# A fixed table of order and engines in place of a list scheduler, in a fused attention and MLP kernel

## The chip, the cores and the metric

The kernel runs on one core of one Trainium2 chip. The metric is the device time of one execution in microseconds (us). An execution can fall in a slow state, more than 1.5% above the fastest run of the same kernel; only fast runs are compared here.

The names used: PE is the matrix engine, DVE, ACT and POOL are the vector, scalar and general engines, SP is the engine that here only issues DMAs. Each engine works through its own instructions in the order in which the program emitted them. In the lines of the profile, `qk` is q and k as loaded, `qkb` their cast, `qkT` the transpose; `pm`, `pt` and `px` are products with w_phi, `EB`, `ea` and `eax` their exponentials, `m` and `mx` maxima; `kv` and `num` are products of attention, `hT_ps` and `ch_ps` the two products of the MLP. PSUM is the memory that takes PE's products.

## The reference

Linear attention with a feature map of exponentials, then a LayerNorm MLP with a residual. Cut to what matters:

```python
# q, k, v: 8 batches x 8 heads x 576 x 64;  w_phi: 64 x 128
def phi(x):
    proj = x @ w_phi
    proj = proj - max(abs(proj))                    # over the 128 features
    return concat(exp(proj), exp(-proj))
kv, z = phi(k).T @ v, phi(k).sum(over s)
x = (phi(q) @ kv) / (phi(q) @ z + 1e-6)             # heads side by side: 8 x 576 x 512
xn = (x - mean(x)) / sqrt(var(x) + 1e-6) * g_ln
out = x + relu(xn @ w_ch1) @ w_ch2                  # 512 -> 2048 -> 512
```

## The kernel before

The work is cut into 32 units (one head of a pair of batches, or a like amount of two heads in the first pair) and the MLP of four pairs of batches. For the first 8 units q and k are transposed on PE; for the other 24 they are cast to bf16 on one of three engines and transposed by a DMA that SP issues. All of it is written as 2513 small operations, each with the engines that may do it, a guessed time on each, and the keys that it reads and writes:

```python
# one unit of pairs 1 to 3: the cast, then the DMA transpose
def cast(e):
    u["qkb"] = att.tile([P, 2, MX * D], BF16, tag="qkb", name="qkb")
    copy_on(e, u["qkb"], qk_bufs[g % NBUF][:, :, u["uu"], :])
def turn():
    u["qkT"] = att.tile([P, 1024], BF16, tag="qkT", name="qkT", bufs=NQ)
    nc.sync.dma_start_transpose(out=..., in_=...)                          # cut
add_any({"POOL": 1.0, "ACT": 0.95, "DVE": 0.8}, V, cast,
        r=main_keys(u, "k") + main_keys(u, "q"), w=[("qkb", n % 2)])        # two buffers
add("SP", 1.27, V, turn, r=[("qkb", n % 2)], w=[("turn", n), *ks], ...)

# MLP: the relu that empties PSUM has two engines, the scaling of w1 by g_ln one
add_any({"ACT": 0.08 + cols * 0.32 / 384, "DVE": 0.08 + cols * 0.4 / 384}, V - 30.0,
        relu, r=[key], w=[hkey[r, jj]], release=[("B", 1)])
add("DVE", 0.9, rank, emit, r=["gln"], w=[("w1", n, kc) for kc in range(KC)])
```

The list scheduler runs the operations through a small simulation with those guessed times and emits them in the order, and on the engines, that come out:

```python
class Order:
    def due(self): ...     # backward pass: gives each operation its rank
    def run(self):         # forward pass, cut
        while events:
            now = events[0][0]
            ...
            for engine, queue in waiting.items():
                if free[engine] > now + 1e-9 or not queue:
                    continue
                ...        # the operation of best rank whose buffers are free
                us = op.alts[engine]
                free[engine] = now + us
                done.append((op, engine))
                ...
        for op, engine in done:
            if op.emit:
                op.emit(engine)
```

Two things follow. An operation with several engines goes to one of them when the program is built. And the two `qkb` buffers are used in turn, so a cast must wait until the transpose of two units earlier has read its buffer; while it waits, everything behind it on its engine waits too. The Trainium skill ("TensorE: Matmul & The Clock Gate", Architectural detail) says that ACT and DVE are strict FIFO; the traces here agree, with a clear case in the experiments (in e5, DVE idle for 4.52 us ahead of a cast that waited for its load).

Of the kernel before, what the change touches and what calls it, by code (L numbers as in the profile page):

```python
# [3 lines left out]

# [16 lines left out]
    return dataclasses.replace(ap, ap=new_ap)  # L21


LAG = {"PE": 0.24, "DVE": 0.20, "ACT": 0.23, "POOL": 0.22, "SP": 0.1, "DMA": 1.8, "CAST": 1.8}


STAY = 10.0


class Op:  # L30
    __slots__ = (
        "alts", "emit", "rank", "lag", "users", "acquire", "release",
        "ready", "left", "number", "rows", "taken", "at", "early",
    )


class Order:


    def __init__(self, room):  # L40
        self.ops, self.wrote, self.read, self.room = [], {}, {}, dict(room)

    def add(
        self, alts, rank, emit, r=(), w=(), acquire=None, release=None, lag=None, rows=False,
        early=0.0
    ):
        op = Op()
        op.alts, op.emit, op.rank, op.lag = alts, emit, rank, lag
        op.early = early
        op.acquire, op.release, op.rows, op.taken = acquire, release, rows, False  # L50
        op.number, op.users, op.ready, op.at = len(self.ops), [], 0.0, None
        deps = {self.wrote[k].number: self.wrote[k] for k in (*r, *w) if k in self.wrote}
        for k in w:
            deps.update({o.number: o for o in self.read.get(k, ())})
        for o in deps.values():
            o.users.append(op)
        op.left = len(deps)
        for k in w:
            self.wrote[k], self.read[k] = op, []
        for k in r:  # L60
            self.read.setdefault(k, []).append(op)
        self.ops.append(op)
        return op

    def due(self):

        waiting, free, events = {}, {}, []
        before, left, ready = {}, {}, {}
        for op in self.ops:
            left[op.number], ready[op.number] = len(op.users), 0.0  # L70
            for o in op.users:
                before.setdefault(o.number, []).append(op)
            for engine in op.alts:
                waiting.setdefault(engine, [])
                free.setdefault(engine, 0.0)
            if not op.users:
                heapq.heappush(events, (0.0, op.number, op))
        rank, taken = {}, set()
        while events:
            now = events[0][0]  # L80
            while events and events[0][0] <= now + 1e-9:
                op = heapq.heappop(events)[2]
                if op is not None:
                    for engine in op.alts:
                        heapq.heappush(waiting[engine], (-op.rank, -op.number, op))
            for engine, queue in waiting.items():
                if free[engine] > now + 1e-9:
                    continue
                op = None
                while queue and op is None:  # L90
                    op = heapq.heappop(queue)[2]
                    if op.number in taken:
                        op = None
                if op is None:
                    continue
                taken.add(op.number)
                end = now + op.alts[engine]
                free[engine], rank[op.number] = end, -end
                heapq.heappush(events, (end, -1, None))
                for o in before.get(op.number, ()):  # L100
                    lag = max(LAG[e] for e in o.alts) if o.lag is None else o.lag
                    same = len(o.alts) == 1 and engine in o.alts
                    n = o.number
                    ready[n] = max(ready[n], end + (0.1 if same else lag))
                    left[n] -= 1
                    if not left[n]:
                        heapq.heappush(events, (ready[n], n, o))
        for op in self.ops:
            op.rank = rank[op.number] - op.early

    def run(self):
        waiting, free, room, events, done = {}, {}, self.room, [], []
        rows = False

        def offer(op):
            heapq.heappush(events, (op.ready, 1, op.number, op, None))

        for op in self.ops:
            for engine in op.alts:
                waiting.setdefault(engine, [])  # L120
                free.setdefault(engine, 0.0)
            if not op.left:
                offer(op)
        now = 0.0
        while events:
            now = events[0][0]
            while events and events[0][0] <= now + 1e-9:
                _, kind, _, op, _ = heapq.heappop(events)
                if kind == 1:
                    for engine in op.alts:  # L130
                        key = op.ready if engine in ("DMA", "CAST") else op.rank
                        heapq.heappush(waiting[engine], (key, op.number, op))
                elif kind == 0:
                    for name, n in op.release or ():
                        room[name] += n
            for engine, queue in waiting.items():
                if free[engine] > now + 1e-9 or not queue:
                    continue
                passed, held, op = [], set(), None
                if engine == "PE" and rows:  # L140
                    near = sorted(i for i in queue if i[2].rows and not i[2].taken)
                    near = [i for i in near if room[i[2].acquire[0]] >= i[2].acquire[1]]
                    if near and near[0][0] < queue[0][0] + STAY:
                        op = near[0][2]
                while queue and op is None:
                    item = heapq.heappop(queue)
                    op = item[2]
                    if op.taken:
                        op = None
                        continue  # L150
                    if op.acquire is None or (
                        op.acquire[0] not in held and room[op.acquire[0]] >= op.acquire[1]
                    ):
                        break
                    held.add(op.acquire[0])
                    passed.append(item)
                    op = None
                for item in passed:
                    heapq.heappush(queue, item)
                if op is None:  # L160
                    continue
                op.taken, op.at = True, (now, engine)
                if op.acquire:
                    room[op.acquire[0]] -= op.acquire[1]
                us = op.alts[engine]
                if engine == "DMA" and free.get("CAST", 0.0) > now:
                    shared = free["CAST"] - now
                    us = 4.0 * us if 4.0 * us <= shared else us + shared * 0.75
                end = now + us
                if engine == "PE" and op.rows != rows:  # L170
                    rows = op.rows
                    end += 0.1
                lag = LAG[engine] if op.lag is None else op.lag
                free[engine] = end
                done.append((op, engine))
                heapq.heappush(events, (end, 2, op.number, op, None))
                heapq.heappush(events, (end + lag, 0, op.number, op, None))
                for o in op.users:
                    same = len(o.alts) == 1 and engine in o.alts
                    o.ready = max(o.ready, end + (0.1 if same else lag))  # L180
                    o.left -= 1
                    if not o.left:
                        offer(o)
        assert len(done) == len(self.ops)
        for op, engine in done:
            if op.emit:
                op.emit(engine)
        return now


@with_exitstack
def kernel(
# [64 lines left out]
    sched = Order({"B": 8, "S": 8})  # L257
# [336 lines left out]
    def a_side(u, i, V):  # L594
# [10 lines left out]
        def em():  # L605
            if i:
                t_ = u["emk_g"]
            elif u["pair"]:
                t_ = u["emq_g"]
            else:  # L610
                if uu == 0:
                    t_ = att_sm.tile([P, 2, NT], FP32, tag="emq", name="emq")
                    group_units(g)[0]["emq_g"] = group_units(g)[1]["emq_g"] = t_
                t_ = u["emq_g"]
# [6 lines left out]
        w = [("em", i, n % 3)]  # L621
# [632 lines left out]
                pass  # L1254
    ET = mybir.EngineType
    with tc.manual_schedule(engines={ET.PE, ET.DVE, ET.Activation, ET.Pool, ET.SP}):
        sched.due()
        sched.run()


# [28 lines left out]
```

## Time and profile before

| | before |
|---|---|
| time, median of 4 runs | 377.43 us (376.82 to 377.68) |
| PE busy | 349.1 us, 93% |
| DVE / ACT / POOL busy | 273.1 / 257.5 / 182.4 us |
| PE idle, 0 to 100 us | 17.1 us (82.90 busy) |
| PE idle, 100 to 360 us | 4.6 us (255.38 busy) |

The page of the kernel before: its span, the busy time of each engine, and the clock and DMA rows of its 40 slices (each 9.4 us long).

```profile
span 375.2 us, 9069 instructions
...
PE 349.1 (93%) x3306; PEld 208.0 (55%) x3348; DVE 273.1 (73%) x738; ACT 257.5 (69%) x650; POOL 182.4 (49%) x349
...
PEclk9998799999999999999999999999999999999998
DMA  6999699999969745493547754712200244010102
```

(This trace lacks 42 matmul records, 36 of them between 100 and 360 us, so PE's busy time in it is a little low.)

### The profile page before, as it was taken

The page shows a single profiled execution, that of the slowest core. Times are in us where ns is not written, and L with a number is a line of the kernel's source. Part 1 is how long each engine was busy: PE and PEld are TensorE (multiplying, and loading weights), DVE is VectorE, ACT ScalarE, POOL GpSimd, SP SyncE. Part 2 cuts the span into 40 slices and gives each one's busy share as a digit, 9 for nine tenths or more (in the row PEclk, how much of TensorE's full clock was granted, in tenths as well). Part 3 has the DMA queues.
Part 4 walks back from the last instruction along what each step waited for, and adds up shares of the span by engine and source line. Part 5 has one row for each costly group of instructions (what it writes and reads, how often), then busy time and mean ns, then how long its engine had stood idle before and what let it go on. Part 6 is the DMA issues. An engine that isn't in the chain of part 4 may idle for free.

```text
span 375.2 us, 9069 instructions
## 1 busy us (share of the span) xinstructions
PE 349.1 (93%) x3306; PEld 208.0 (55%) x3348; DVE 273.1 (73%) x738; ACT 257.5 (69%) x650; POOL 182.4 (49%) x349
## 2 busy tenths in 40 slices
PE   2888789989999899999999999999999999999995
PEld 1466456546565555655656555655565546555553
DVE  3889989979879999987879979978788672000102
ACT  3889698799879648876569768966589437433310
POOL 5589989367866434744455537454447320000000
PEclk9998799999999999999999999999999999999998
DMA  6999699999969745493547754712200244010102
GB/s 174 291 281 192 124 223 265 239 233 234 256 145 242 221 114 119 84 237 106 189 141 159 208 130 99 152 39 72 66 2 28 58 114 98 9 48 29 56 30 84
DMA packets 89132, 52.43 MB, mean 140 GB/s; under 512 B 55552, under 2 KB 84608, under 8 KB 89088
## 3 DMA queue, kind: packets, MB, share of 16 engines
q1 hardware_dynamic: 84240, 47.11, 50.9%
q0 software_dynamic: 4224, 4.19, 7.0%
q10 hardware_dynamic: 624, 0.56, 0.5%
q8 instruction: 26, 0.43, 0.5%
q14 instruction: 18, 0.15, 0.1%
HBM read 36.77 MB, written 9.44 MB: 123 GB/s over the span
## 4 chain that ended last, share of the span: by engine, by line
PE 74%; DVE 9%; DMA 6%; ACT 6%; issue 2%; POOL 2%; SPq 0%; DVEq 0%; POOLq 0%
PE ch_ps L1033 30%; PE hT_ps L1001 29%; DMA qkT<-qkb 4%; PE num L738 4%; PE kv L709 4%; PE pm L580 3%; ACT EB L631 3%; DVE m L600 3%; DMA qk<-in_k_dram 2%; ACT ea L684 1%; PE pt L678 1%; DVE numc L744 1%; DVE numc L750 1%; PE kv L704 1%; DVE st L881 1%
## 5 line engine op out<-in xcount | busy, mean ns | idle before, releaser
L1001 PE MATMUL hT_ps<-xT,w 128*128 128x384 bf16 x768 | 150.7, 328 | 1.5 <-DVE m L600 1.0
L1033 PE MATMUL ch_ps<-w,hT 128*128 128x512 bf16 (+2 forms) x550 | 141.0, 373 | 2.7 <-issue 0.9
L1001 PEld LDWEIGHTS <-w 128*128 128x128 bf16 x768 | 71.4, 98 | 54.7 <-issue 5.2
L1011 ACT ACTIVATE hT<-hT_ps 128x384 bf16<-128x384 f32 x119 | 58.5, 496 | 58.9 <-PE hT_ps L1001 58.4
L600 DVE TENSOR_REDUCE m<-pm 128x4 f32<-128x512 f32 x128 | 81.4, 676 | 9.0 <-PE pm L580 8.9
L762 POOL TENSOR_TENSOR x<-numc,rden 128x192 bf16<-128x192 f32 (+1 forms) x112 | 50.4, 461 | 67.4 <-DVE rden L756 65.2
L1033 PEld LDWEIGHTS <-hT 128*128 128x128 bf16 x592 | 53.3, 98 | 47.0 <-issue 2.5
L684 ACT ACTIVATE ea<-pt 128x512 bf16<-128x512 f32 x128 | 69.0, 637 | 7.2 <-PE pt L678 7.1
L631 ACT ACTIVATE EB<-pm 128x512 bf16<-128x512 f32 x128 | 69.0, 634 | 3.0 <-DVE m L600 2.6
L1041 DVE SCALAR_TENSOR_TENSOR o<-ch_ps,rstd,x 128x512 f32<-128x512 f32 (+2 forms) x37 | 26.6, 727 | 54.6 <-PE ch_ps L1033 39.5
L645 POOL TENSOR_TENSOR vv<-v,emk 128x512 bf16<-128x512 f32 x32 | 33.5, 1047 | 43.9 <-ACT emk L616 33.3
L1009 DVE TENSOR_SCALAR hT<-hT_ps 128x384 bf16<-128x384 f32 x73 | 39.0, 542 | 4.9 <-PE hT_ps L1001 4.3
L744 DVE TENSOR_TENSOR numc<-num,emq 128x195 f32<-128x195 f32 (+1 forms) x96 | 32.4, 344 | 10.1 <-PE num L738 8.9
L738 PEld LDWEIGHTS <-ea 128*128 128x128 bf16 x512 | 28.0, 99 | 13.7 <-issue 1.9
L750 DVE TENSOR_TENSOR numc<-numc,num 128x195 f32<-128x195 f32 (+1 forms) x100 | 33.1, 342 | 1.2
L645 POOL TENSOR_TENSOR vv<-v,en 128x512 bf16<-128x512 f32 x32 | 33.5, 1047 | 0.0
L738 PE MATMUL num<-KV,ea 128*128 128x65 bf16 x512 | 31.8, 196 | 1.1 <-ACT ea L684 0.9
L881 DVE BATCH_NORM_STATS2 st<-x 128x6 f32<-128x512 bf16 x36 | 24.4, 677 | 2.1 <-POOL x L762 1.9
L709 PE MATMUL kv<-vv,EB 128*128 128x65 bf16 x512 | 25.0, 199 | 0.0
L580 PEld LDWEIGHTS <-qkT 64*128 64x128 bf16 x512 | 16.8, 99 | 14.2 <-issue 8.2
L890 ACT ACTIVATE xc<-x,mv 128x512 bf16<-128x512 bf16 x19 | 13.8, 725 | 14.6 <-DVE mv L882 12.2
L709 PEld LDWEIGHTS <-EB 128*128 128x128 bf16 x512 | 22.6, 102 | 1.6
(71 smaller groups left out, 371.3 us busy)
## 6 DMA issues: line engine op xcount, KB each, us to landing
out_dram<-o SPq DMA_DIRECT2D x31, 256.0 KB, 2.4
qk<-in_k_dram SPq DMA_DIRECT2D x28, 256.0 KB, 4.6
v<-in_v_dram SPq DMA_DIRECT2D x28, 256.0 KB, 3.7
qk<-in_q_dram SPq DMA_DIRECT2D x26, 256.0 KB, 5.2
w<-in_moe_w_ch_dram POOLq DMA_DIRECT2D x8, 512.0 KB, 9.4
qk<-in_k_dram SPq DMA_DIRECT2D x2, 512.0 KB, 6.8
qk<-in_q_dram SPq DMA_DIRECT2D x2, 512.0 KB, 7.8
v<-in_v_dram SPq DMA_DIRECT2D x2, 512.0 KB, 8.2
```

Of the source, the lines that this page charges most:

```text
L600: nc.vector.reduce_max(out=u["m", i].rearrange("p (c e) -> p e c", e=2)[:, e], in_=u["pm", i, e], axis=AX.X, apply_absolute_value=True,)
L631: nc.scalar.activation(u["EB"][:, t, e * 4 : (e + 1) * 4].rearrange("p c f -> p (c f)"), u["pm", 1, e].rearrange("p c f -> p (c f)"), AF.E ...
L645: nc.gpsimd.tensor_tensor(out=u["vv"][:, t, 0:MX, 0:D], in0=vb[:, uu, :].rearrange("p (c d) -> p c d", d=D), in1=bcast(e[:, 0:MX], 2, D), ...
L684: nc.scalar.activation(u["EA"][:, t, e * 512 : (e + 1) * 512], u["pt", e], AF.Exp, scale=(1.0, -1.0)[t],)
L709: nc.tensor.matmul(ps[:, t, c // 4, :], EB[:, t, (c % 2) * 4 + c // 2, :], vv[:, t, c, :], start=False, stop=(t == 0 and c == MX - 1), ski ...
L738: nc.tensor.matmul(ps[:, t, i, :], lhsT, rhs, start=(j == 0), stop=(j == len(terms) - 1))
L750: nc.vector.tensor_add(out=st["numc"][:, 0:nch], in0=st["numc"][:, 0:nch], in1=st["ps"][:, 0])
L762: nc.gpsimd.tensor_tensor(out=dst, in0=st["numc"][:, i : i + cnt, 0:D], in1=bcast(st["rden"][:, i : i + cnt], 2, D), op=ALU.mult,)
L1001: nc.tensor.matmul(st["ps"][:, 0:cols], w1_sb[:, kc, jj * P : (jj + 1) * P], pr["xT", r][:, kc, 0:cols], start=(kc == 0), stop=(kc == KC - 1),
L1009: nc.vector.tensor_relu(h_sb[:, 0:cols], st["ps"][:, 0:cols])
L1011: nc.scalar.activation(h_sb[:, 0:cols], st["ps"][:, 0:cols], AF.Relu)
L1033: nc.tensor.matmul(ch[t, c0], hT[r, jj][:, rt * P : (rt + 1) * P], w2_sb[:, jj, c0:c1], start=(jj == 0), stop=(jj == JC - 1),)
```

## The change

The intent: a search that was done offline found an order and a choice of engines that are better than what the list scheduler finds while the kernel is built; they are written down as a table and followed. A word of the table is the number of an operation, with a letter for the engine (d, a, p for DVE, ACT, POOL) where it has a choice.

```diff
 class Op:
-    __slots__ = ("alts", "emit", "rank", "lag", "users", ...)
+    __slots__ = ("alts", "emit", "number", "before")
 class Order:
-    def due(self): ...
-    def run(self): ...
+    def follow(self, order):
+        done = set()
+        for number, engine in order:
+            op = self.ops[number]
+            assert op.before <= done and engine in op.alts, number
+            if op.emit:
+                op.emit(engine)
+            done.add(number)
+        assert len(done) == len(self.ops)
+
+WORK = """
+0 6 1 2 4 10 8 7 12 3 5 11 14 9 59 16 13 60 18 36 61a 37 20 15 17 62a 69 19 22 21 78 70 23
+...                                                     (2513 words in all, cut)
+"""
@@ in the maxima of the first pair
-                if uu == 0:
+                if "emq_g" not in u:
@@ at the end
-        sched.due()
-        sched.run()
+        sched.follow(work(sched.ops))
```

Operations and dependences are the same 2513 in both. The edit of the maxima only lets either unit of a group be the first to take the group's tile.

## The prediction

> **What bounds the kernel now.** TensorE, but not everywhere. The page gives PE 349.1 us busy of 375.2 (93%), DVE 273.1, ACT 257.5, POOL 182.4. Busy time by windows of 12.5 us splits this: from 100 to 362 us PE is busy 11.7 to 12.5 of each, bound by its own work. From 12.5 to 62.5 us it is busy 9.9 to 11.6, while ACT (11.8, 11.7, 9.0, 11.6) and DVE (10.4, 11.7, 11.0, 12.5) are nearly full: attention's exponentials and maxima set the pace, and the first MLP matmul starts at 45.5 us (timeline of PE). Counting matmuls at their dense spacing (162 ns for 384 columns, 216 ns for 512, from the timeline) I estimate that PE loses 47 us between its first and last matmul: 25.6 before 45.5, 4.4 to 62.5, 8.9 to 125 (single waits of about 1.1 us near 52, 82 and 124 us), 8.0 after that, mostly 0.3 us at attention pieces that any order pays. Outside stand 3.5 us before the first matmul and 4.3 after the last.
>
> **What the change does.** Nothing is removed or added: the same 2513 operations and dependences, emitted in a table's order. With both orders side by side, PE's is a local shuffle of the old one (attention progress per MLP work is the same within about 1 us). Engine choices move: 8 of the 24 bf16 casts of q and k go from ACT or DVE to POOL, as do 7 centerings; 38 of 73 relus of DVE go to ACT, 27 come back. At durations near the trace's (relu 496 ns on ACT, 542 on DVE) DVE loses about 6 us of work, POOL gains 7, ACT is unchanged.
>
> **On the critical path.** Little before 45.5 us: the work ordered ahead of the first MLP matmul even grows (DVE 33.3 to 35.7 us, ACT 33.6 to 35.2, POOL 26.0 to 29.6), so it should start at 45 to 47.5 us. Ahead of the last third of the first pair's MLP DVE's share falls from 82.7 to 78.2 us, where DVE is 96% full: worth up to 4 us, at most the PE loss there. I count 1.5 us gained to 62.5, 3.5 from there to 125, 2 after: 7 us. The MLP end is already dense; the tail of 4.3 us is unchanged.
>
> A side condition is the clock: the windows show 0.86 and 0.73 granted in 25 to 50 us. The Trainium skill ("TensorE: Matmul & The Clock Gate", the HAM clock gate) says that the clock is halved after an idle window of about 3.4 us, free-running; this trace agrees in form (half clock for 3.4 and 6.8 us). A denser early PE may save, a shifted one lose, 1 to 3 us.
>
> **Predicted: 370.5 us**, 365.5 to 376 eight times in ten. Faster by over 2%: 0.42; within 2%: 0.54; slower: 0.04.
>
> **What would show it.** PE busy share 94 to 95%; DVE busy about 267, POOL about 189; PE's waits at 75 to 88 and 112 to 125 us shrunk; first MLP matmul no earlier than 45 us; last 60 us unchanged.
>
> **What would make it wrong.** A table tuned on a model that misses POOL's or the PSUM rotation's real waits would turn its tight order into stalls (slower). If the search also advanced the first MLP matmul by several us, the gain exceeds 10 us.

## More of the kernel before

PE is nearly full after 100 us, so what can still be won lies in the first quarter, where the DMA row stands at 9 as well.

The view by windows (busy time and count of PE, PEld, DVE, ACT and POOL, granted clock, DMA share, GB/s) splits that quarter:

```profile
70.00:75.00 5.00, 4.71 (x38) 2.27 (x37) 4.93 (x13) 4.84 (x10) 2.22 (x3) 1.00 0.93 254
75.00:88.00 13.00, 11.28 (x138) 6.88 (x137) 10.91 (x28) 11.97 (x32) 8.79 (x16) 1.00 1.14 234
```

From 70 to 88 us PE idles for 2.0 us while ACT is busy for 16.8 of 18. The chain of waits in that stretch shows with what (start, length, what):

```profile
61.53 10.27 DMA qkT<-qkb
...
71.82 1.04 ACT qkb L289
...
72.97 0.93 ACT qkb L289
73.91 0.98 ACT EB L631 x2
...
75.10 4.91 DMA qkT<-qkb
80.00 1.92 issue
81.93 0.86 DVE qkb L291
```

Two casts (`qkb`) take 2 us of ACT ahead of the exponentials (`EB`). A third sits on DVE. The timelines of DVE and PE there:

```profile
81.93 0.86 DVE L291 CAST qkb<-qk 128x1024 bf16<-128x1024 f32 x1 [1.92 <-issue]
82.71 1.01 DVE L1009 TENSOR_SCALAR hT<-hT_ps 128x384 bf16<-128x384 f32 x2
83.31 0.96 PE L947 MATMUL xT_ps<-ident,xc 128*128 128x128 bf16 x12 [0.91 <-DVE hT L1009]
```

Before its cast DVE sits idle for 1.92 us, until the transpose that reads this cast's buffer has landed (issued at 75.10, landed at 81.85, behind loads of q, k and v; the profile names no releaser, "issue"), two relus come late behind it, and PE waits 0.91 us for them. Last, the start of PE:

```profile
3.53 0.61 PE L550 MATMUL qkT_ps<-ident,qk 128*128 128x128 bf16 x4 [3.53 <-DMA qk<-in_k_dram]
5.67 0.61 PE L550 MATMUL qkT_ps<-ident,qk 128*128 128x128 bf16 x4 [1.53 <-DMA qk<-in_q_dram]
6.95 0.61 PE L580 MATMUL pm<-wbk,qkT 64*128 64x128 bf16 x8 [0.68 <-ACT qkT L289]
```

## The result, and the profile after

| | before | after |
|---|---|---|
| time, median of 4 runs | 377.43 us (376.82 to 377.68) | 373.21 us (372.68 to 374.35) |
| ratio | | 0.9895, 95% interval 0.9868 to 0.9922: within 2% |
| PE idle, 0 to 100 us | 17.1 us | 13.9 us (86.10 busy) |
| PE idle, 100 to 360 us | 4.6 us | 3.0 us (256.98 busy) |

A ratio here is the mean time of one kernel's fast runs over the mean of the other's fast runs of the same rounds, so it is not quite the ratio of the medians that stand beside it. The fall from 4.6 to 3.0 us after 100 us is not read as a gain, since the trace before lacks records there and the one after lacks none. The page after:

```profile
span 371.1 us, 9107 instructions
...
PE 349.6 (94%) x3348; PEld 208.1 (56%) x3348; DVE 266.8 (72%) x728; ACT 257.5 (69%) x653; POOL 187.9 (51%) x356
...
PEclk9998799999999999999999999999999999999998
```

The same windows of the kernel after:

```profile
70.00:75.00 5.00, 5.00 (x46) 2.14 (x44) 4.93 (x12) 4.97 (x14) 3.12 (x5) 1.00 1.09 342
75.00:88.00 13.00, 12.95 (x154) 7.81 (x152) 12.27 (x32) 12.95 (x34) 12.10 (x23) 1.00 1.09 234
```

From 70 to 88 us PE's idle time fell from 2.0 to 0.05 us. The chain there holds no cast and no transpose, only ACT's own exponentials and then PE:

```profile
72.21 0.54 ACT eax L484 x2
72.75 0.97 ACT EB L638 x2
...
73.82 0.97 ACT EB L638 x2
74.79 1.96 ACT ea L691 x4
...
76.80 0.37 PE pt L685
```

The casts of these units are now on POOL (POOL's timeline):

```profile
68.97 1.04 POOL L298 CAST qkb<-qk 128x1024 bf16<-128x1024 f32 x1
...
72.56 1.04 POOL L298 CAST qkb<-qk 128x1024 bf16<-128x1024 f32 x1
...
78.40 1.03 POOL L298 CAST qkb<-qk 128x1024 bf16<-128x1024 f32 x1
```

In the start, the first load of q goes out ahead of the second load of the phi weights on ACT's queue, both batches of transposes run at once, and the first product with phi comes 0.87 us sooner:

```profile
4.37 1.03 PE L557 MATMUL qkT_ps<-ident,qk 128*128 128x128 bf16 x8 [4.37 <-POOL vx L1151]
6.08 0.61 PE L587 MATMUL pm<-wbk,qkT 64*128 64x128 bf16 x8 [0.68 <-DVE wbq L1159]
```

One wait of this kind did not shrink but grew. PE waited 0.97 us for a DVE maximum at 125.7 us before, and 1.51 us at 117 us after (PE, then DVE):

```profile
116.95 0.81 PE L1008 MATMUL hT_ps<-xT,w 128*128 128x384 bf16 x4 [1.51 <-ACT EB L638]
112.29 2.89 DVE L405 TENSOR_SCALAR w<-w,gln 128x512 bf16<-128x512 bf16 x4
```

One chunk of the scaling of w1 holds DVE for 2.89 us (2.37 in the kernel before), where the operation's guessed time is 0.9 us, and maxima that ACT and then PE need stand behind it.

**Where the time went.** The two programs do the same work on PE in nearly the same order, so I give each weight load the time of its matmul at dense spacing (322 us in all) and ask when PE had come to a given amount of that work. The difference to the kernel before, in us (negative is ahead), one profiled execution each, experiments included:

| PE's work done, us (time before) | 10 (32.3) | 40 (74.8) | 50 (88.7) | 100 (142.9) | 319 (366.6) |
|---|---|---|---|---|---|
| after | −1.4 | −1.7 | −4.1 | −4.5 | −4.4 |
| e1 old order, new engines | −0.9 | +0.4 | −1.4 | +2.7 | +6.5 |
| e2 new order, old engines | −1.0 | +1.0 | +0.1 | +2.2 | +5.7 |
| e3 table to 97 us | −1.6 | −2.1 | −5.1 | −4.5 | −4.5 |
| e4 table from 97 us | +0.4 | +0.2 | +0.3 | −0.4 | −1.1 |
| e5 old order, w2 early | +0.3 | +2.5 | +1.8 | +1.5 | +1.5 |
| e6 table, w2 late | −1.8 | −2.9 | −5.4 | −6.3 | −6.4 |
| e7 old order, q first | −0.9 | −2.3 | −2.2 | −2.2 | −1.4 |
| e8 table from 68 us | −1.1 | −1.8 | −4.3 | −0.4 | −0.3 |
| e9 old order, casts on POOL | −0.3 | −0.3 | −1.2 | −1.4 | −1.4 |
| e10 table, casts back | −1.1 | +0.7 | −0.6 | −0.9 | −0.4 |
| e11 old order, q first and casts | −0.8 | −1.1 | −2.2 | −0.5 | −0.5 |
| e12 table, two moves | −1.6 | −1.3 | −3.8 | −4.9 | −5.0 |

In the changed kernel a lead of 1.5 us is there after the first 9 us, it grows by 2.5 us between 75 and 89 us, and then stands. The last 278 us add nothing that this one execution shows. A row is one execution, and executions of one kernel differ by 1 to 5 us (before: 375.2 to 379.9 in the last batch), so only steps of about a microsecond in one place are read from it. The clock is a part of that scatter: between 21 and 51 us the traces record half clock for 10.2 us in most rows and in the kernel before, but for 13.7 in e1 and e9, 6.8 in e5, e6 and e12, and 3.4 in e3. Up to 97 us e3 emits just what the table does, so its larger lead there (−2.1 and −5.1) is chance.

### The profile page after: what moved, and what is told of

It is laid out like the page before. It is cut to its first block, busy times and chain, and to the rows that moved or that the text cites. A ratio compares the mean times of both kernels' runs of the same rounds, so it can differ in the third digit from the quotient of the medians.

```text
span 371.1 us, 9107 instructions
## 1 busy us (share of the span) xinstructions
PE 349.6 (94%) x3348; PEld 208.1 (56%) x3348; DVE 266.8 (72%) x728; ACT 257.5 (69%) x653; POOL 187.9 (51%) x356
## 4 chain that ended last, share of the span: by engine, by line
PE 77%; ACT 10%; DVE 5%; DMA 4%; issue 1%; POOL 1%; SPq 0%; DVEq 0%; POOLq 0%; ACTq 0%
PE hT_ps L1008 32%; PE ch_ps L1040 28%; PE num L745 4%; PE kv L716 4%; ACT EB L638 3%; PE pm L587 3%; ACT ea L691 3%; PE pt L685 2%; DMA qk<-in_k_dram 1%; DMA qkT<-qkb 1%; PE kv L711 1%; PE qkT_ps L557 1%; DVE w L405 1%; DMA xT<-xc 1%; DVE st L888 1%
## 5 line engine op out<-in xcount | busy, mean ns | idle before, releaser
L1008 PE MATMUL hT_ps<-xT,w 128*128 128x384 bf16 x768 | 144.8, 327 | 2.6 <-ACT EB L638 1.9
L1040 PE MATMUL ch_ps<-w,hT 128*128 128x512 bf16 (+1 forms) x592 | 146.7, 373 | 0.0
L1018 ACT ACTIVATE hT<-hT_ps 128x384 bf16<-128x384 f32 x130 | 63.6, 503 | 58.4 <-PE hT_ps L1008 57.7
L1040 PEld LDWEIGHTS <-hT 128*128 128x128 bf16 x592 | 52.3, 98 | 45.9 <-issue 1.0
L691 ACT ACTIVATE ea<-pt 128x512 bf16<-128x512 f32 x128 | 67.9, 620 | 10.4 <-PE pt L685 10.3
L638 ACT ACTIVATE EB<-pm 128x512 bf16<-128x512 f32 x128 | 70.1, 632 | 5.3 <-DVE m L607 5.3
L1016 DVE TENSOR_SCALAR hT<-hT_ps 128x384 bf16<-128x384 f32 x62 | 33.4, 549 | 3.5 <-PE hT_ps L1008 3.2
L745 PE MATMUL num<-KV,ea 128*128 128x65 bf16 x512 | 30.5, 195 | 1.2 <-ACT ea L691 0.5
L587 PEld LDWEIGHTS <-qkT 64*128 64x128 bf16 x512 | 17.6, 99 | 13.8 <-issue 8.3
L298 POOL CAST qkb<-qk 128x1024 bf16<-128x1024 f32 x14 | 15.1, 1076 | 13.3 <-DMA qkT<-qkb 11.3
```

Source lines behind the costliest of these rows:

```text
L638: nc.scalar.activation(u["EB"][:, t, e * 4 : (e + 1) * 4].rearrange("p c f -> p (c f)"), u["pm", 1, e].rearrange("p c f -> p (c f)"), AF.E ...
L691: nc.scalar.activation(u["EA"][:, t, e * 512 : (e + 1) * 512], u["pt", e], AF.Exp, scale=(1.0, -1.0)[t],)
L745: nc.tensor.matmul(ps[:, t, i, :], lhsT, rhs, start=(j == 0), stop=(j == len(terms) - 1))
L1008: nc.tensor.matmul(st["ps"][:, 0:cols], w1_sb[:, kc, jj * P : (jj + 1) * P], pr["xT", r][:, kc, 0:cols], start=(kc == 0), stop=(kc == KC - 1),
L1016: nc.vector.tensor_relu(h_sb[:, 0:cols], st["ps"][:, 0:cols])
L1018: nc.scalar.activation(h_sb[:, 0:cols], st["ps"][:, 0:cols], AF.Relu)
```

## The experiments

To splice the two, I wrote the list scheduler's own result down as a table of the same form; that kernel is the same as the one before, instruction for instruction. All kernels here are correct. Those sent together ran on the same chip with the kernel before: the first four beside 377.82 us, the next four beside 377.20, the last four beside 377.05 (medians of 11).

The theories at the start: P, the whole gain arises before 97 us; against it, that it is spread over the run, or that it comes from the engine letters alone or the order alone.

### e1: the old order with the table's engines

```diff
 for number in LIST_ORDER:
-    engine = list scheduler's
+    engine = table's
```

> The list scheduler's order, written as a table, with the table's engine for every operation that has a choice (casts, relus, centerings, small copies). Theory E (the gain is the engine choice: DVE's 6 us go to POOL, casts no longer block DVE near 80 us): 373 to 374.5 us, and PE's wait near 83 us is gone. Theory O (the gain is the order on PE and the other queues): 377 to 378 us. Both half: 375.5.

Measured: 383.41 us (382.11 to 384.87), ratio 1.0149 (1.0119 to 1.0178): slower than both.

### e2: the table's order with the old engines

```diff
 for number in TABLE_ORDER:
-    engine = table's
+    engine = list scheduler's
```

> The mirror of e1: the table's order with the list scheduler's engine choice. Theory E: 376.5 to 378 us. Theory O: 373 to 374. If neither part works alone (the order was found for these engines), both e1 and e2 are at 376 us or above.

Measured: 381.06 us (378.56 to 383.00), ratio 1.0088 (1.0048 to 1.0127): slower than before.

Neither half of the change carries a part of the gain over the whole run: each alone costs 3 to 6 us. An engine choice fits only the order that it was made with; where e1 and e2 lose was not traced beyond the table above (e1 goes from −1.4 us at 89 us to +6.5 at the end). In the stretch from 70 to 88 us, though, PE's idle time is 0.8 us with the new engines in the old order and 2.4 us with the old engines in the new order (before 2.0, by the windows): there the engines matter more.

### e3: the table up to 60 us of PE's work (about 97 us), then the list order

```diff
-order = TABLE
+order = TABLE[up to 60 us of PE work] + rest in list order, with the list's engines
```

> The table up to 60 us of PE work (about 97 us of the run), then the list scheduler's order for all that is left. Theory P (the PE progress curves of the two traces part only before 9 us, by 1.5 us, and between 74 and 88 us, by 2.5 to 3 us, and run parallel afterwards): all of the gain, 373 to 374 us. Rival D (the gain is spread, and later stretches of the table add to it or need to fit to its start): 375 us or above.

Measured: 374.08 us (372.88 to 375.53), ratio 0.9905 (0.9879 to 0.9931): nearly all of the gain (0.9895).

### e4: the list order up to that point, then the table

```diff
-order = LIST
+order = LIST[up to 60 us of PE work] + rest in the table's order, with its engines
```

> The list scheduler's order up to 60 us of PE work, then the table. Theory P: no gain, 377 to 378 us. Rival D: a part of the gain, 375 to 376 us.

Measured: 376.18 us (375.23 to 377.08), ratio 0.9961 (0.9938 to 0.9983). The time lies between what P (377 to 378) and D (375 to 376) expected, nearer to D. The interval leaves out 1: the table's later part gains some 1.5 us behind an old first part, between 163 and 250 us in the trace. In the changed kernel that gain does not show. Theory P stands for the change as a whole (e3); the small later gain of e4 is not explained.

The next question was what in the first 97 us does it. Three candidates: W, the loads of w2 go out 3.7 to 4.7 us sooner in the table, and the transposes that were behind them with it; S, the start (q first); and H, the casts: where a cast stands on a busy engine, the engine loses its time, or blocks if the cast's buffer is still being read.

### e5: the old order, the loads of w2 as early as in the table

```diff
-... 324 ... 326 ... 396 ... 398        (the four load issues on POOL)
+324 325 326 327 moved ahead of 272;  396 397 398 399 moved ahead of 394
-            r=after, w=[("w2", jj) for jj in range(j0, j1)],      (a gate that held these loads back)
+            r=[], w=[("w2", jj) for jj in range(j0, j1)],         (the same for w1)
```

> The list scheduler's order and engines; only the issues of the last four weight loads (w2) are moved forward in POOL's order, so that they leave at about 41.5 and 51 us in place of 46 and 54 us. Theory W (the 2.5 to 3 us that the table gains between 74 and 88 us come from these loads leaving the shared DMA engines 4 us sooner, so that the q/k transposes queued behind them land sooner): 374.5 to 375.5 us, transposes near 62 us land by 69 us in place of 71.8. Rival C (the gain comes from the order and engine of casts and of PE's work in that stretch itself): 377 to 378.5 us.

Measured: 378.38 us (377.33 to 380.41), ratio 1.0029 (0.9998 to 1.0059). The loads did land 7 us sooner (61.8 in place of 68.9 us), but then a load of q landed later, and the cast waiting for it blocked DVE:

```profile
63.07 0.69 DVE L289 CAST qkb<-qk 128x1024 bf16<-128x1024 f32 x1 [4.52 <-DMA qk<-in_q_dram]
```

PE waited 2.5 us for what stood behind this cast. The load of q that this cast needed was issued at 53.13 us and landed at 63.05 (before: 47.69 and 58.01). The view by windows has the DMA engines full there (a share of 1.21 from 50 to 63 us), so in this case a transfer that was moved forward pushed another one back. The Trainium skill ("DMA: Bandwidth & Descriptors", Issuing engines are not separate DMA queues) says that DMAs from whatever engine end up on the same 16 DMA engines and interleave; this trade between POOL's queue and SP's agrees.

### e6: the table, the loads of w2 late

```diff
+326 327 324 325 moved behind 394;  398 399 396 397 moved behind 448   (and the same gate dropped)
```

> The mirror of e5: the table with these four loads moved back on POOL by about 4 us, to where the list scheduler's run issued them. Theory W: 375.5 to 376.5 us. Rival C: 373 to 374.

Measured: 373.28 us (median of the five fast runs, 370.88 to 374.32; one slow run of 378.76 is left out), ratio 0.9891 (0.9858 to 0.9925): the same as the table. Against theory W this is weaker than it looks: the loads went out 3.4 to 3.9 us later than in the table, but the last of them landed only 0.8 us later (65.35 us; table 64.59, before 68.9). The better test of W is e8.

### e7: the old order, the first load of q ahead of the phi weights

```diff
-0 2 1 6 4 10 8 3 7 12 5 11 ...
+0 6 1 2 4 10 8 3 7 12 5 11 ...
```

> The list scheduler's order with one exchange: ACT's queue issues the first q load ahead of its half of w_phi, as the table does. Theory S (this exchange is what starts PE's work earlier: the second batch of transposes no longer waits for q until 5.7 us): the first product of q and k at about 6.1 us in place of 6.95, and 376.5 to 377 us. Rival L (the earlier start is luck in when the first loads land): 377.5 to 378.5 us.

Measured: 376.73 us (375.31 to 378.58), ratio 0.9980 (0.9947 to 1.0013). In the trace the first product with phi moves from 6.95 to 5.80 us, and PE is 0.9 us ahead at 10 us of work. In the time the gain is not resolved. The start also differs by chance: the executions with the old order of these two loads reached the first 1 us of work at 0, −0.9, +0.4, +0.5, −1.1 and −0.1 us against the kernel before (itself, e1, e4, e5, e8, e9; mean −0.2), and the eight with q first (after, e2, e3, e6, e7, e10, e11, e12) at −0.6 to −1.7 us (mean −1.2). Clearer is the start of the first product with phi: 5.81 to 6.49 us in the eight executions with q first, 6.86 to 7.86 us in the six without, with no overlap. So theory S is right in the traces and rival L is not; the start is worth about 1 us.

### e8: the list order up to 34 us of PE's work (about 68 us), then the table

```diff
-order = LIST
+order = LIST[up to 34 us of PE work] + rest in the table's order, with its engines
```

> The list scheduler's order up to 34 us of PE work (about 68 us of the run, all weight loads issued), then the table. Theory W: no more than the switch at 97 us gave (376.2), 376 to 377.5 us, since the weights left late. Rival C: the table's stretch from 74 to 88 us gives its 2.5 us, 374 to 375 us.

Measured: 376.88 us (median of the five fast runs, 373.84 to 377.65; one slow run of 380.75 is left out), ratio 0.9960 (0.9921 to 1.0000). By the time alone this is what theory W expected. The trace says otherwise: the last load of w2 landed at 66.93 us and the two transposes behind it at 70.43 and 71.33 (before 68.9, 71.80 and 72.70; table 64.59, 68.81 and 70.40; about as far ahead of the kernel before as PE itself was by then, 1.8 us), and yet the trace gains 2.5 us in the stretch from 75 to 89 us, like the table. So that gain does not need the early loads, and with e5 theory W falls. Right after, the trace loses nearly 4 us. The reason is a cast once more, this time on ACT; the lines are from the timelines of ACT and PE and from the view by windows:

```profile
92.55 1.04 ACT L288 CAST qkb<-qk 128x1024 bf16<-128x1024 f32 x1 [5.08 <-POOL x L761]
94.13 0.29 PE L703 MATMUL kv<-vv,EBx 128*128 128x130 bf16 x1 [2.56 <-ACT hT L1010]
93.90:97.30 3.40, 3.17 (x30) 1.94 (x32) 0.22 (x1) 2.99 (x8) 0.82 (x1) 0.50 1.00 290
```

ACT sat idle for 5.08 us ahead of a cast whose buffer was read by a transpose until 92.37 us (the profile names POOL, which came earlier); relus and exponentials stood behind it, PE waited 2.56 us, and its clock was at half for the next 3.4 us. A table that fits its own past does not fit another one.

The last four test theory H on the three casts of the stretch (units 10, 11, 12; before on ACT, ACT, DVE, in the table all on POOL) against R: where they sit does not matter, the order does.

### e9: the old order, the three casts on POOL

```diff
-... 766a ... 826a ... 862d ...
+... 766p ... 826p ... 862p ...
```

> The list scheduler's order and engines, except that three casts of q and k (the 11th, 12th and 13th unit's, u10, u11 from ACT and u12 from DVE) go to POOL, as in the table. Theory H (a cast that waits for a DMA transpose blocks the in-order engine it sits on; on POOL that costs nothing, on DVE and ACT it delays relus and exponentials that PE waits for between 74 and 88 us): 375 to 376 us, 1.5 to 2 us gained in that stretch, DVE no longer idle 1.92 us at 80 to 82 us. Rival R (where these casts sit does not matter, the table's order does): 377 to 378 us, the same as before.

Measured: 376.60 us (375.46 to 378.52), ratio 0.9993 (0.9955 to 1.0031): no gain that the time can show, and not the 1.5 to 2 us expected. The trace gains 0.9 us between 40 and 50 us of work. The view by windows and ACT's timeline show why not more:

```profile
70.00:75.00 5.00, 5.00 (x40) 2.31 (x37) 4.93 (x13) 3.27 (x8) 4.11 (x5) 1.00 1.01 277
75.00:88.00 13.00, 11.93 (x154) 7.54 (x154) 12.05 (x31) 12.97 (x37) 9.79 (x19) 1.00 1.15 254
72.67 0.21 ACT L452 ACTIVATE emk<-mx 128x2 f32<-128x2 f32 x1 [0.89 <-DVE mx L440]
73.60 1.09 ACT L629 ACTIVATE EB<-pm 128x512 bf16<-128x512 f32 x2 [0.72 <-DVE m L598]
```

DVE's 1.92 us of idle are gone, and ACT is rid of 2 us of casts. But ACT then waits 1.61 us in the same place for maxima (0.89 and 0.72); the list order has no other work for it between. In the table ACT has other work between the same two points, a centering, two steps of `rstd` and the exponentials of the short tiles (from 71.05 to 72.64 us), and runs from 70 to 77 us with no gap; in the list order the last of these come 12 us later, at 83.7 us, and PE waits 0.34 us for them there. So the time that was freed turned into a wait.

### e10: the table, the three casts back on ACT, ACT and DVE

```diff
-... 766p ... 826p ... 862p ...
+... 766a ... 826a ... 862d ...
```

> The table's order and engines, except that the same three casts go back to the engines that the list scheduler gave them (u10, u11 to ACT, u12 to DVE). Theory H: 1.5 to 3 us lost between 74 and 100 us, 375 to 376.5 us, with an idle gap on ACT or DVE ahead of a cast. Rival R: 373 to 374 us, the same as the table.

Measured: 375.88 us (373.56 to 376.67), ratio 0.9964 (0.9924 to 1.0003), where the table has 0.9895 (0.9868 to 0.9922). The difference of the ratios, 0.0069, is 2.6 us of the table's 4; the two intervals together allow about 0.8 to 4.4 us (my estimate). In the same rounds on the same chip e12, the table with two other moves, took 371.92 us. Its windows and its chain of waits:

```profile
70.00:75.00 5.00, 4.30 (x39) 1.98 (x37) 4.90 (x14) 4.72 (x13) 1.44 (x3) 1.00 1.17 282
75.00:88.00 13.00, 12.03 (x138) 6.94 (x138) 10.99 (x29) 12.90 (x32) 9.86 (x17) 1.00 1.00 242
72.42 1.06 ACT qkb L288
73.48 0.62 ACT xc L889
...
75.07 0.97 ACT EB L630 x2
76.05 0.93 ACT qkb L288
...
77.09 0.97 ACT EB L630 x2
```

PE idles for 1.7 us from 70 to 88 us again (0.05 in the table). Theory R falls: three letters out of the table cost, by the means, more than half of what the whole table gains. But the form of H has to be corrected too. I expected an idle gap ahead of a cast, and there is none here: the two casts simply take 1.06 and 0.93 us of ACT in a stretch in which ACT sets the pace, as the chain shows. Of the loss in the trace since the kernels part, some 2.1 us (from 1.4 us behind the table at 36 us of work to 3.5 us behind at 50), these two are nearly all.

### e11: the old order with q first and the three casts on POOL

```diff
-0 2 1 6 4 10 ...    766a ... 826a ... 862d
+0 6 1 2 4 10 ...    766p ... 826p ... 862p
```

> The run with the list order and the three casts on POOL, and the first load of q ahead of the phi weights on ACT's queue besides. Theories H and S together (start 0.9 us sooner, casts 1.5 to 2 us): 374 to 375.3 us, most of the table's gain from four edits. Rival R: 376.5 to 377.2 us, from the start alone.

Measured: 375.78 us (374.09 to 376.72), ratio 0.9962 (0.9921 to 1.0003): about a third of the table's gain (0.0038 of 0.0105), not most of it, and not resolved from none. The trace is 2.2 us ahead at 50 us of work and gives 1.7 back before 100 us of time: POOL, with the casts added, is late with products of v, and PE waits for it twice, 0.58 and 1.02 us.

### e12: the table with two operations moved later

```diff
-985 1092 1054 751 694 1378p        (second chunk of the w1 scaling, on DVE)
+985 1092 1054 694 1378p ... 703 1029 992 751 1077      (behind the maxima)
-1422 1582p 1459                    (a cast on POOL that blocks it for 6.10 us)
+1422 1459 ... 1464 1435 1582p 1583 (behind a product of v)
```

> The table with two operations moved later on their engine: the second chunk of the scaling of w1 on DVE behind the maxima that PE waits for near 115 us (PE waits 1.5 us there under the table), and the cast on POOL that waits 6 us for a transpose near 167 us behind the product of v that PE waits 1.2 us for. If both waits shrink and nothing else moves: 371 to 372.5 us, a version faster than both. If the waits only move on: 373 to 373.7 us, the same as the table.

Measured: 371.92 us (371.33 to 373.02), ratio 0.9871 (0.9836 to 0.9905). This is the lowest time of all and within what was expected. Every one of its six runs is below the median of the changed kernel, but those ran in other rounds than these, and the intervals of the two ratios overlap: that it beats the table is likely, not shown. In its trace the waits of 1.51 us at 117 and 1.2 us at 172 us are gone; a wait of 0.76 us for maxima at 120 us is new.

## Why the prediction was right or wrong

The time (373.21 us) lies in the predicted range, 2.7 us above the value, and the class "within 2%" was the likelier one.

- **PE bounds, with its slack before 125 us: right.** PE's share rose from 93% to 94%, and all of the gain that the trace shows lies before 100 us. The last 60 us are unchanged, as predicted.
- **Loads of the engines: right.** Predicted DVE about 267, POOL about 189, ACT unchanged; measured 266.8, 187.9, 257.5 (before 257.5).
- **Little before 45.5 us, first MLP product at 45 to 47.5 us: right.** It came at 46.4 us (before 45.5).
- **The gain by stretch, "1.5 us gained to 62.5, 3.5 from there to 125, 2 after": the terms were mis-sized.** Measured on the progress of PE: 1.5 us, all of it in the first 9 (about 1 by the order of two loads, the rest within what executions differ by); about 3 from there to 143 us; nothing after. The sum was 7, and it is 4.4 in the trace and 4.2 in the medians. The failed term is the 2 us after 125, taken from the 8 us that PE loses there: e3 has nearly the whole gain without that part of the table. I had written that most of that loss is 0.3 us at pieces "that any order pays", and counted a quarter of it as a gain nevertheless.
- **"DVE's share falls from 82.7 to 78.2 us, where DVE is 96% full": the reason for the middle term was wrong, its size about right.** The load of DVE over the stretch is not what PE waited for. From 70 to 80 us ACT sets the pace, and what the table takes from it is two casts (e10); one more cast blocked DVE for 1.92 us by waiting, not by working. Old order with the new, lighter DVE load is 1.5% slower (e1). I did not move the relus by themselves, so what they are worth is open.
- **Waits at 75 to 88 us and at 112 to 125 us shrunk: half right.** PE's idle time in the first fell from 1.72 to 0.05 us. The wait in the second went from 0.97 to 1.51 us; the scaling of w1 takes 2.89 us where its guessed time is 0.9.
- **The clock: neither saved nor lost, as far as it is recorded.** Both traces record half clock for 3.4 us near 31 us and for 6.8 us near 42 us. But the record of the clock begins only at 24.84 us (before) and 23.97 us (after), and the 1.00 that the views print ahead of that is no measurement. PE's transposes at 4.37 us (after, shown above) and at 3.53 us (before) start 107 ns apart, as in the recorded half clock, against 56 ns at full clock, so PE began at half pace in both kernels. The timeline of PE in the kernel before, in full and in half clock:

```profile
30.01 0.61 PE L550 MATMUL qkT_ps<-ident,qk 128*128 128x128 bf16 x8 [0.31 <-ACT ea L684]
34.15 1.01 PE L550 MATMUL qkT_ps<-ident,qk 128*128 128x128 bf16 x8
```

What stays open: without three letters the table loses, by the means, more than half of its gain (e10), but in the old order the same letters bring little that the time can show (e9, e11); the order around them supplies the rest, and I showed one place of it (what ACT has in line at 71 us). The other parts of that fit are not separated. The gain of e4 after 163 us is not explained either, nor are the losses of e1 and e2.

## What to carry to other kernels

In this kernel, whose engines take their work in order, the place of a job that could be done anywhere (a cast) was worth more than the balance of busy times: keep such a job off the engine that paces the stretch, and where it has to wait for a DMA, put it on the engine with slack. Order and engine choice were found together and work only together: either without the other made the kernel slower, and time freed on one engine turned into a wait where the order had nothing ready to fill it. Read the gain by where PE gets ahead, not by busy shares; here 4 us came from two stretches of 9 and 14 us, and 278 us added nothing that shows.

## What the Trainium skill lacked or had wrong

- "TensorE: Matmul & The Clock Gate", What's actually happening (the HAM clock gate): half clock is said to come after at least one idle window of about 3.4 us. Here it followed a PE wait of 2.56 us (e8), and in the kernel before it began at 31.67 us although the single waits of PE in the 4 us ahead of it were at most 0.72 us; the 3.67 us ahead of it had 2.06 us of busy PE, 0.61 us of it transposes on PE (whether these count like other products is not tested here; first line below, the half clock in the second, from the view by windows of the kernel before). The page's section A second HAM failure mode, with small idle times between groups, is closer to this, but it gives no number for how little work is enough.

```profile
28.00:31.67 3.67, 2.06 (x37) 1.58 (x37) 3.56 (x13) 3.67 (x13) 3.67 (x9) 1.00 1.15 206
31.67:35.08 3.41, 3.29 (x34) 2.52 (x34) 3.06 (x13) 3.12 (x10) 3.40 (x7) 0.50 1.18 179
```

- The same page, Back-to-back issue gap: its formula gives 216 ns for 512 columns, and calls that too high for a real stream, with about 131 ns sustained. The trace of e12 shows the formula's value in the dense stream: three products of 512 columns in 0.65 us, 217 ns each, and four of 384 columns in 0.65 us, 162 ns each (chain of waits):

```profile
177.50 0.65 PE ch_ps L1032 x3
178.15 0.65 PE hT_ps L1000 x4
```

- "DMA: Bandwidth & Descriptors", DMA Transpose (X-bar): no number for how long a transpose takes to land beside other loads. From 64 to 90 us it took 4.8 to 10.3 us from issue to landing in the kernel before (median 6.6) and 3.7 to 6.4 us after (median 4.9), and this is what a cast waits for.
